# An S5 state-space layer and a SwiGLU layer side by side: the first chunk's state output as seven block products, and the up half-columns in two pairs at other places

## The chip, the cores and the metric

The kernel runs on one core of a Trainium2 chip. The metric is the device time of one execution in microseconds (us). TensorE (PE in the profile) multiplies matrices, VectorE (DVE) and ScalarE (ACT) do elementwise work, GpSimd (POOL) issues DMAs that add into their target and does a few small powers, and SyncE (SP) issues loads, stores and transposing DMAs.

## What is computed

The input `x` has 2048 rows (time steps) of 512 features. With `xn` the layer norm of `x`, the output is `x` plus an S5 state-space layer of `xn` plus a SwiGLU layer of `xn`:

```python
Bu = einsum("bld,pd->blp", xn, B_bar)            # complex, 512 states
h_t = Lam_bar * h_{t-1} + Bu_t                   # along the 2048 steps
y  = 2 * einsum("blp,dp->bld", h, C).real + xn * Dskip
f  = (silu(xn @ w_gate) * (xn @ w_up)) @ w_down  # F = 1376
out = x + y + f
```

## The kernel before

The 2048 rows are worked in four chunks of 512 columns (`NCH`, `CW`), each of four tiles of 128 rows. `xnT` holds `xn` transposed. For chunks 2 and 3 ACT normalizes the rows (L235) with a factor that is a power on POOL (L214) and a shift `nb` from DVE (L217), both once for a chunk; DMAs transpose the result. Ten products of constants (L828) run on PE before its first data. For each chunk there are these stages:

- **B projection** (`bproj_chunk`, products at L380): eight banks of PSUM, real and imaginary part of four state tiles. ACT casts each bank into `u` (L382).
- **State** (`ssm_ops`), on DVE: `u` is rotated by cosine and sine tables `c16` and `s16`, so that the recurrence becomes real; eight scans (L459); a small carry (L468 to L473); and a rotation back into the state `wt`. `rotation` has four products and two sums on DVE. `rotation_dma` has the four products alone, and POOL issues two DMAs that add one product into another (L426); it needs the negated sine table, which `negate_table` makes with four copies on ACT (L411).
- **Gate and up** (`gateup_chunk`): first the last feature tile (L550, evicted by L553 and L554), then ten feature tiles, each with a gate and an up bank (L492), evicted by ACT with silu (L511) and a cast (L512). DVE multiplies two tiles at a time (L507).
- **Last feature tile.** Of its 96 columns, 96 of gate and 32 of up are in the bank of L550. The other 64 columns of up are made for all four chunks at once by `up_halves` (L539), two chunks in a bank. DVE multiplies (L527), and `move_rows` has SP issue 12 small DMAs for each chunk that lay the product out for `out_rows` (L595).
- **Output** (`out_ffn`, L750, or L724 for the last pair): a PSUM bank for each tile of 128 rows gathers the products with `w_down`, then `out_rows`, then the state part.

The state part multiplies the state (real and imaginary) by C folded with its coefficients, `CF`. `CF` is made by `c_ops`: eight times a scaled copy on ACT (L363) and a DVE step (L366). There are two forms. `out_ssm` has 8 products of 512 columns for each tile (L762), 32 for a chunk. `out_ssm_seven` treats state and `CF` as 2 x 2 blocks and makes the product of a chunk from seven block products of 256 columns (L657, 56 products), by Winograd's form of Strassen's scheme. It needs sums of blocks. Those of `CF` (`t1` to `t4`, in place of `CT`) and those of the state (`s1` to `s4`) are made by signed copies on ACT (L606) and adding DMAs from POOL (L610), each in a chain of dependent steps. Two results go through ACT (L690, L693), and four adds and four final sums are on DVE (L669). Before, chunk 0 and chunk 3 use `out_ssm` and chunks 1 and 2 the seven products.

**What sets the order.** Each engine runs its instructions in the order in which the program gives them, and the program is written out by hand: the stages of PE follow each other as above, and the DVE work stands in a list, `backlog`, of steps with a cost. After each PE group `pump` adds the group's time to what is owed and takes steps from the list; `need(tag)` empties the list up to a tag; `multiply` takes waiting products; `spend` takes steps from the list `sums`. Where a step stands in the list therefore decides where it stands in each engine's queue. PE's order from the middle on is: gate and up of chunk 1, B projection of chunk 2, output of chunk 0 with `up_halves` and `out_ssm`, gate and up of chunk 2, B projection of chunk 3, output of chunk 1 with the seven products, gate and up of chunk 3, and `out_pair` for chunks 2 and 3. There are eight PSUM banks. The four output banks of chunk 0 stay taken from its output products until its last row products, which come with the output of chunk 1.

Of the kernel before, what the change touches and what calls it, by code (L numbers as in the profile page):

```python
# [23 lines left out]
def kernel(  # L24
# [382 lines left out]
    neg_s16 = xnT[:, :, 0:CW]  # L407

    def negate_table():
        for q in range(NQ):  # L410
            nc.scalar.activation(out=neg_s16[:, q], in_=s16[:, q], func=ACT.Copy, scale=-1.0)  # L411

    def rotation_dma(src, dst, back):

        box = {}
        sines = (s16[:], neg_s16) if back else (neg_s16, s16[:])

        def side(i):
            t = box[i] = ssm.tile([128, NQ, CW], BF16, name="pm", bufs=3)
            V.tensor_tensor(out=t[:], in0=src()[:, i], in1=sines[i], op=ALU.mult)  # L420
# [22 lines left out]
    def ssm_ops(c):  # L443
# [9 lines left out]
        ops = (rotation_dma if c == 3 else rotation)(lambda: u_tiles[c], lambda: u_tiles[c], False)  # L453
# [27 lines left out]
        back = (rotation_dma if c == 2 else rotation)(g, wt, True)  # L481
# [4 lines left out]
    u_pair = {}  # L486
    products = []
# [12 lines left out]
    def u_tile(c, fi):  # L500
        if (c, fi // 2) not in u_pair:
            u_pair[c, fi // 2] = up_p.tile([128, 2, CW], BF16, name="u2")
        return u_pair[c, fi // 2]

    def product(c, fi):
        g, u = gu_tile(c)[:, fi - 1:fi + 1, :], u_tile(c, fi)[:]
# [16 lines left out]
    def product_last(c):  # L523
        g, u = gu_last[c % 2][0:LB + LA, :], ul(c)[0:LB + LA, :]
        def mul():
            to = g if c == NCH - 1 else u
            V.tensor_tensor(out=to, in0=g, in1=u, op=ALU.mult)  # L527
            move_rows(c, to)
        products.append(mul)

    def up_halves():

        pss = []
        for c in range(0, NCH, 2):
            ps = bank()
            pss.append(ps)
            for k in range(KD):
                for i in range(2):
                    nc.tensor.matmul(ps[i * LB:(i + 1) * LB], lhsT=wu_last[:, k, :],  # L539
                                     rhs=xnT[:, k, (c + i) * CW:(c + i + 1) * CW], start=(k == 0), stop=(k == KD - 1))  # L540
        for c in range(NCH):
            i = c % 2
            nc.scalar.copy(out=ul(c)[0:LB, :], in_=pss[c // 2][i * LB:(i + 1) * LB])
        product_last(0)
        product_last(1)

    def gateup_last(c):
# [7 lines left out]
        if c > 1:  # L555
            product_last(c)
# [18 lines left out]
    def skip_add():  # L575
        V.tensor_tensor(out=xn_end[:], in0=xn_end[:], in1=xall[:, NT - TPC:NT, :], op=ALU.add)
# [23 lines left out]
    neg_b22 = BT[:, 1, :, 0:HD]  # L600
    parts = {NT - 1: part_end, NT - 2: jidx}

    def signed_copy(out, in_, sign):

        for lo in range(0, NQ, 2):
            yield lambda lo=lo: nc.scalar.activation(out=out[:, lo:lo + 2], in_=in_[:, lo:lo + 2], func=ACT.Copy,  # L606
                                                     scale=sign)

    def added(out, in_):
        yield lambda: nc.gpsimd.dma_start(out=out, in_=in_, accum_op=ALU.add)  # L610

    def weight_sums():
# [3 lines left out]
        for out, in_, sign, to, add in ((t3, b12, -1.0, t3, b22), (t1, b11, -1.0, t1, b12), (t2, b11, 1.0, t2, t3),  # L616
                                        (t4, b22, -1.0, t4, t1)):
            yield from signed_copy(out, in_, sign)
            yield from added(to, add)
        yield from added(t4, b21)  # L620
# [6 lines left out]

    def state_sums(c):

        (a11, a12), (a21, a22) = state_quarters(c)  # L630
        if c == 1:
            s1, s2, s3 = (ssm.tile([128, NQ, HW], BF16, name="cm", bufs=3) for _ in range(3))
            s4 = jidx[:].bitcast(BF16).rearrange("p (q j) -> p q j", q=NQ)
        else:
            s1, s2, s3, s4 = ((wg_g, wu_g)[i // 2][2][:, :, (i % 2) * HD:(i % 2 + 1) * HD] for i in range(4))
        s_tiles[c] = (s1, s2, s3, s4)
        for out, in_, sign, to, add in ((s1, a21, 1.0, s1, a22), (s3, a21, -1.0, s3, a11), (s2, a11, -1.0, s2, s1),
                                        (s4, a12, -1.0, s4, s2)):
# [471 lines left out]
```

## Time and profile before

| | us |
|---|---|
| three runs | 176.61, 176.98, 176.90 |
| median | 176.9 |
| profiled execution | 177.04 |
| its span, first to last instruction | 175.2 |
| PE busy | 171.7 (98%) |
| DVE busy | 161.1 (92%) |
| ACT busy | 107.6 (61%) |
| POOL busy | 45.9 (26%) |

PE's granted clock was 1.00 in the whole execution. In the chain of waits each piece is the work that the next piece waited for, back from the last instruction; in the timelines a row gives the start, the time from first start to last end, engine, line, operation, tiles and count, and in brackets how long the engine stood idle before it and what released it. The DMA view gives for each kind of transfer the size of one and the median time from issue to landing.

### The profile page before, as it was taken

The numbers are of one execution on the slowest core, as the hardware profiler recorded it, in microseconds if no ns is written. First come the engines' busy times: TensorE is split into PE (matmuls) and PEld (weight loads), VectorE is DVE, ScalarE is ACT, GpSimd is POOL, SyncE is SP. The second block draws the span as 40 slices with busy tenths as digits, with TensorE's granted clock in tenths as the row PEclk, the third lists the DMA queues.
The fourth block names the chain that finished last, engine by engine and source line by source line (L and its number), as shares of the span: only waits on it lengthen the run. The fifth ranks groups of instructions, "written<-read, shape, count | busy, mean of one in ns | idle before, by whom it ended". The sixth has DMA issues, their size and how long they took to land.

```text
span 175.2 us, 2790 instructions
## 1 busy us (share of the span) xinstructions
PE 171.7 (98%) x1002; PEld 88.4 (50%) x1002; DVE 161.1 (92%) x248; ACT 107.6 (61%) x204; POOL 45.9 (26%) x49
## 2 busy tenths in 40 slices
PE   8999999999999999999999999999999999999993
PEld 2977544444444444444444444468444444447743
DVE  4779998999999997999999999999999999995884
ACT  5487898868598669772998699052486691001100
POOL 6050120000400130000352224136544841211440
PEclk9999999999999999999999999999999999999999
DMA  6998496995332013700399449339898999955034
GB/s 170 294 170 226 91 250 117 362 230 121 77 76 30 0 30 75 254 4 11 43 105 120 60 51 194 61 60 136 139 156 153 157 175 192 122 60 60 0 105 139
DMA packets 38974, 21.36 MB, mean 122 GB/s; under 512 B 22016, under 2 KB 38144, under 8 KB 38944
## 3 DMA queue, kind: packets, MB, share of 16 engines
q0 software_dynamic: 9552, 8.26, 34.0%
q1 hardware_dynamic: 28016, 12.30, 31.1%
q10 hardware_dynamic: 1392, 0.62, 1.3%
q8 instruction: 8, 0.13, 0.3%
q14 instruction: 6, 0.05, 0.1%
HBM read 8.33 MB, written 4.19 MB: 71 GB/s over the span
## 4 chain that ended last, share of the span: by engine, by line
PE 98%; DVE 0%; issue 0%
PE ps L492 35%; PE ps L380 16%; PE ps L724 10%; PE ps L750 10%; PE ps L762 8%; PE ps L657 7%; PE ps L851 2%; PE ps L828 2%; PE ps L550 2%; PE ps L932 2%; PE ps L595 2%; PE ps L539 1%; PE ps L245 1%; DVE res L767 0%; PE ps L275 0%
## 5 line engine op out<-in xcount | busy, mean ns | idle before, releaser
L492 PE MATMUL ps<-xnT,wg 128*128 128x512 bf16 (+1 forms) x148 | 36.6, 373 | 0.0
L492 PE MATMUL ps<-xnT,wu 128*128 128x512 bf16 (+1 forms) x148 | 36.6, 373 | 0.0
L459 DVE TENSOR_TENSOR_SCAN g<-r_t,car,u 128x512 bf16<-128x512 f32 x24 | 28.7, 1264 | 0.0
L380 PE MATMUL ps<-xnT,BT 128*128 128x512 bf16 x128 | 28.3, 379 | 0.0
L511 ACT ACTIVATE guT<-ps 128x512 bf16<-128x512 f32 (+1 forms) x40 | 24.0, 599 | 5.4 <-PE ps L492 3.4
L512 ACT CAST u<-ps 128x512 bf16<-128x512 f32 (+1 forms) x40 | 23.3, 583 | 4.7 <-PE ps L492 4.5
L492 PEld LDWEIGHTS <-wu 128*128 128x128 bf16 x148 | 14.5, 98 | 16.6
L492 PEld LDWEIGHTS <-wg 128*128 128x128 bf16 x148 | 14.4, 98 | 16.5
L382 ACT CAST u<-ps 128x512 bf16<-128x512 f32 x32 | 18.2, 586 | 4.0 <-PE ps L380 3.9
L380 PEld LDWEIGHTS <-BT 128*128 128x128 bf16 x128 | 12.5, 98 | 14.9
L750 PE MATMUL ps<-wd_sb,guT 128*128 128x512 bf16 x80 | 17.6, 379 | 0.0
L724 PE MATMUL ps<-wd_sb,guT 128*128 128x512 bf16 x80 | 17.4, 379 | 0.0
L214 POOL TENSOR_TENSOR rstd<-ve,neg_half 128x2 f32<-128x2 f32 (+1 forms) x4 | 5.7, 1415 | 44.9 <-DVE ve L213 44.9
L762 PE MATMUL ps<-CF,wt 128*128 128x512 bf16 (+2 forms) x80 | 14.2, 336 | 0.0
L507 DVE TENSOR_TENSOR guT<-guT,u 128x1024 bf16<-128x1024 bf16 x20 | 13.4, 679 | 0.0
L724 PEld LDWEIGHTS <-guT 128*128 128x128 bf16 x80 | 7.8, 98 | 9.4
L750 PEld LDWEIGHTS <-guT 128*128 128x128 bf16 x80 | 7.8, 98 | 9.4
L205 DVE BATCH_NORM_STATS2 stats<-xall 128x6 f32<-128x512 bf16 x14 | 9.5, 679 | 2.0 <-DMA xall<-in_A_x_dram 2.0
L610 POOL DMA_DIRECT2D CT<-CF x3 | 3.9, 1300 | 27.1 <-ACT CT L606 23.6
L690 ACT COPY guT<-ps 128x512 f32<-128x512 f32 x2 | 1.2, 586 | 15.8 <-PE ps L657 15.8
L762 PEld LDWEIGHTS <-wt 128*128 128x128 bf16 x80 | 7.1, 98 | 6.9 <-issue 0.4
L459 DVE TENSOR_TENSOR_SCAN g<-r_t,u 128x512 bf16<-128x512 f32 x8 | 9.3, 1205 | 0.0
(168 smaller groups left out, 265.0 us busy)
## 6 DMA issues: line engine op xcount, KB each, us to landing
wd_sb<-in_B_w_down_dram SPq DMA_DIRECT2D x2, 640.0 KB, 8.7
xall<-in_A_x_dram SPq DMA_DIRECT2D x1, 1024.0 KB, 6.2
out_dram<-res POOLq DMA_DIRECT2D x8, 128.0 KB, 3.8
wt<-pm POOLq DMA_DIRECT2D x2, 512.0 KB, 5.4
u<-pm POOLq DMA_DIRECT2D x2, 512.0 KB, 6.2
out_dram<-xall POOLq DMA_DIRECT2D x2, 512.0 KB, 10.2
CT<-CF POOLq DMA_DIRECT2D x3, 256.0 KB, 4.3
gu_rows<-ul SPq DMA_DIRECT2D x36, 8.0 KB, 1.8
```

Source lines behind the costliest of these rows:

```text
L205: nc.vector.bn_stats(out=stats[:, n, :], in_=xall[:, n, :])
L380: nc.tensor.matmul(ps[:], lhsT=BT[:, part, k, q * 128:(q + 1) * 128], rhs=xnT[:, k, c * CW:(c + 1) * CW], start=(k == 0), stop=(k == KD - 1))
L382: nc.scalar.copy(out=u_tiles[c][:, part, q, :], in_=ps[:])
L459: V.tensor_tensor_scan(out=g()[:, part, q, :], data0=r_t[:, q:q + 1].to_broadcast([128, CW]), data1=u_tiles[c][:, part, q, :], initial=ini ...
L492: nc.tensor.matmul(ps[:fs, lo:hi], lhsT=wslice(groups, fi, k), rhs=xnT[:, k, c * CW + lo:c * CW + hi], start=(k == 0), stop=(k == KD - 1))
L507: products.append(lambda: V.tensor_tensor(out=g, in0=g, in1=u, op=ALU.mult))
L511: nc.scalar.activation(out=gu_tile(c)[:, fi, 0:hi], in_=psg[:, 0:hi], func=ACT.Silu)
L512: nc.scalar.copy(out=u_tile(c, fi)[:, fi % 2, 0:hi], in_=psu[:, 0:hi])
L657: nc.tensor.matmul(place(i), lhsT=a[:, q, i * 128:(i + 1) * 128], rhs=b[:, q, :], start=(start and q == 0), stop=(stop and q == NQ - 1))
L724: nc.tensor.matmul(o[:], lhsT=gu_tiles[k][:, fi, i * 128:(i + 1) * 128], rhs=wd_sb[:, fi, :], start=(fi == 0), stop=False)
L750: nc.tensor.matmul(o[:], lhsT=gu_tiles[c][:, fi, i * 128:(i + 1) * 128], rhs=wd_sb[:, fi, lo:hi], start=(fi == 0), stop=False)
L762: nc.tensor.matmul(o, lhsT=w_tiles[c][:, part, q, i * 128:(i + 1) * 128], rhs=CF[:, part, q, lo:hi], start=(fresh and part == 0 and q == 0 ...
```

## The change

- Chunk 0's `out_ssm` goes. Its output banks stay open, and `out_ssm_seven(0)` runs behind the B projection of chunk 3, with chunk 0's row products; the sums of chunk 1's state are written out there too, ahead of it.
- The state sums of chunk 0 start inside the list of `c_ops` (`sums_begin`, after the first C step), and the sums of `CF` follow it (`sums_go_on`, then `leftover`). Signed copies with sign +1 become plain DMA copies from SP (or from ACT's queue for chunk 1); the order of all sums is new, and the last operand is no longer negated separately.
- `up_halves` becomes `up_pair(0)`, ahead of the B projection of chunk 2, and `up_pair(2)`, ahead of that of chunk 3, with their products and row moves.
- Chunk 0's rotation back and chunk 1's rotation forward use `rotation_dma` too. The negated sine table moves to `part_end` and `jidx` and is made during gate and up of chunk 1, one copy for a feature tile.
- `skip_add` becomes an adding DMA; the skip products of the chunks come in the order 3, 2, 0, 1; the stores of chunks 0 and 1 move into `out_pair`, and the state sums of chunk 2 behind its first output tile.
- The copy of `x` to the output moves ahead of `up_pair(0)`, `load_rows` behind the B projection of chunk 3. The up tiles `u2` become slices of one tile `u_all`, whose space chunk 0's seven products use.

The core of the diff:

```diff
-    neg_s16 = xnT[:, :, 0:CW]
+    neg_s16 = [t[:].bitcast(BF16).rearrange("p (q j) -> p q j", q=2) for t in (part_end, jidx)]
...
-        ops = (rotation_dma if c == 3 else rotation)(lambda: u_tiles[c], lambda: u_tiles[c], False)
+        ops = (rotation_dma if c in (1, 3) else rotation)(lambda: u_tiles[c], lambda: u_tiles[c], False)
...
-        back = (rotation_dma if c == 2 else rotation)(g, wt, True)
+        back = (rotation_dma if c in (0, 2) else rotation)(g, wt, True)
...
-    def up_halves():
...
+    def up_pair(c):
+
+        ps = bank()
+        for k in range(KD):
+            for i in range(2):
+                nc.tensor.matmul(ps[i * LB:(i + 1) * LB], lhsT=wu_last[:, k, :],
+                                 rhs=xnT[:, k, (c + i) * CW:(c + i + 1) * CW], start=(k == 0), stop=(k == KD - 1))
+        for i in range(2):
+            nc.scalar.copy(out=ul(c + i)[0:LB, :], in_=ps[i * LB:(i + 1) * LB])
...
     def skip_add():
-        V.tensor_tensor(out=xn_end[:], in0=xn_end[:], in1=xall[:, NT - TPC:NT, :], op=ALU.add)
+        nc.gpsimd.dma_start(out=xn_end[:], in_=xall[:, NT - TPC:NT, :], accum_op=ALU.add)
...
     def weight_sums():
...
+        yield from copied(t4, b21, pieces=2)
+        yield from negated(t1, b11)
+        yield from added(t1, b12)
+        yield None
+        yield from negated(t2, b22)
+        yield from added(t2, t1)
+        yield from negated(t3, b12)
+        yield from added(t3, b22)
+        yield from added(t4, t2)
...
     def state_sums(c):
...
+        s1, s2, s3, s4 = s_tiles[c] = [t[:] for t in state_places(c)]
+        q = nc.scalar if c == 1 else nc.sync
+        yield from negated(s2, a22)
+        yield from copied(s4, a12, q)
+        yield from copied(s1, a21, q)
+        yield from negated(s3, a21)
+        yield from added(s3, a11)
+        yield from added(s1, a22)
+        yield None
+        yield from added(s2, s3)
+        yield from added(s4, s2)
...
     def out_pair(c):
 
         multiply(0)
         for n in [*parts, *range(c * TPC, NT - len(parts))]:
             o_tiles[n] = [bank()]
-        for op in state_sums(c):
-            op()
         for n in range(c * TPC, (c + 2) * TPC):
+            if n == c * TPC + 1:
+                need("skip")
+                for _, op in filter(None, state_sums(c)):
+                    op()
+                skip_store(0)
+                skip_store(1)
...
     def out_chunk(c):
...
         if c == 0:
-            need("ln3")
-            up_halves()
-            negate_table()
-            multiply(0)
-        if c == 1:
-            for step in range(3):
-                for k in range(2):
-                    out_rows(k, step)
-            for n in range(TPC):
-                out_leave(n, o_tiles[n][0], opool.tile([128, D], BF16, name="res"))
+            need("cf")
+            sums.extend(leftover)
+            spend(4)
+            return
+        for k in range(3):
+            out_rows(c, k)
         need(f"ssm{c}")
-        need("cf")
-        if c == 1:
-            spend(99, True)
-            return out_ssm_seven(c)
-        for n in range(c * TPC, (c + 1) * TPC):
-            out_ssm(n)
-            pump(2 * NQ * 0.2163)
+        out_ssm_seven(c)
...
-    fwd1, back1, _ = ssm_ops(1)
-    queue("ssm1", fwd1 + back1)
+    fwd1, back1, turns = ssm_ops(1)
+    queue("ssm1", fwd1[:turns])
...
+    cf = c_ops()
+    queue("cf", cf[:1] + [(0.0, sums_begin)] + cf[1:] + [(0.0, sums_go_on)])
+    queue("ssm1", fwd1[turns:] + back1)
+    sums += negate_table()
     gateup_chunk(1)
+    nc.sync.dma_start(out=out[0, 0:(NT - 2 * TPC) * 128, :], in_=A_x[0, 0:(NT - 2 * TPC) * 128, :])
+    up_pair(0)
+    product_last(0)
+    product_last(1)
     nc.gpsimd.dma_start(out=dsk_bc[:], in_=A_Dskip.partition_broadcast(128))
     bproj_chunk(2)
-    nc.sync.dma_start(out=out[0, 0:(NT - 2 * TPC) * 128, :], in_=A_x[0, 0:(NT - 2 * TPC) * 128, :])
     queue_ssm(2)
     out_chunk(0)
-    sums += [*weight_sums(), None]
     gateup_chunk(2)
+    up_pair(2)
+    product_last(2)
     bproj_chunk(3)
+    load_rows()
+    need("ssm1")
+    spend(99)
+    sums.extend(filter(None, state_sums(1)))
+    spend(99)
+    out_ssm_seven(0)
+    move_rows(2, ul(2))
```

More of the change, by code (lines that the diff above doesn't have):

```diff
@@ L962, with spend @@
     sums = []
-    def spend(n, late=False):
-        while n and sums:
-            if sums[0] is None:
-                if not late or any(item[3] == "ssm1" for item in backlog):
-                    return
-                sums[0:1] = state_sums(1)
-            sums.pop(0)()
-            n -= 1
+    def spend(n):
+        while sums and sums[0][0] <= n:
+            cost, op = sums.pop(0)
+            op()
+            n -= cost
     def bproj_chunk(c):
```

129 lines of the change are left out of this document (63 added, 66 removed).

## The prediction

> **What bounds the kernel now.** I read the page's busy shares first, then the chain of waits in order of time, then the timelines of ScalarE (ACT), VectorE (DVE), GpSimd (POOL) and the DMA queue of SyncE around the places that the change touches. In the chain each row is start, length, engine, tile, line, count.
>
> ```profile
> PE 171.7 (98%) x1002; PEld 88.4 (50%) x1002; DVE 161.1 (92%) x248; ACT 107.6 (61%) x204; POOL 45.9 (26%) x49
> ```
> ```profile
> 56.70 6.91 PE ps L380 x32
> 63.60 8.63 PE ps L750 x40
> 72.24 1.85 PE ps L539 x16
> 74.09 7.01 PE ps L762 x32
> ...
> 81.96 17.27 PE ps L492 x80
> ...
> 116.17 6.22 PE ps L657 x56
> ...
> 140.53 17.27 PE ps L724 x80
> 157.79 1.41 PE ps L595 x24
> 159.20 6.36 PE ps L657 x56
> ```
>
> The chain is TensorE (PE) alone, one stage beginning where the last ended: it has no gap. Whatever is saved on PE is saved outright, and every gap that a change opens is paid in full. DVE is the second bound: 161.1 us of work, and at the end only just ahead (below). The sum is made against the profiled execution, 177.04 us with a span of 175.2; the median of the runs shown is 176.9, 0.14 lower, and I end on that.
>
> **What the change saves on PE.** Chunk 0's state output was 32 products of 512 columns, 7.01 us (L762). Seven block products are 56 of 256 columns; the kernel already has them for chunk 1, 6.22 us, and chunk 2, 6.36 us. Saved: 7.01 - 6.22 = 0.79 us. The up half-columns (L539, 16 products, 1.85) become two pairs of 8, 0.92 each: nothing gained or lost. The third pass of the row products (L595) is regrouped, not changed. So the change can give 0.8 us; the question is whether PE stays without a gap.
>
> **Where PE comes to wait: the start of chunk 2's gate and up.** Before, 1.85 + 7.01 us of PE work lay between the output products of chunk 0 (L750) and gate and up of chunk 2, and ACT used them to catch up. Both are gone from there. By the new order PE ends gate and up of chunk 1 at 56.70 as now, runs the first up pair to 57.62, the B projection (6.91) to 64.53, the output products (8.63) to 73.16, and starts chunk 2 at once. Four of the eight PSUM banks hold chunk 0's unfinished outputs until the seven products, so four are left: the last feature tile, gate 0, up 0 and gate 1 take them, four times 4 x 0.216 = 0.86 us, until 76.6. Up 1 takes the bank of the last feature tile, and waits for ACT to have emptied it. ACT's queue is in order, so I follow what stands before that.
>
> ```profile
> 56.93 1.22 DVE L390 TENSOR_TENSOR pm<-g,c 128x2048 bf16<-128x2048 bf16 x1
> 58.06 0.68 DVE L205 BATCH_NORM_STATS2 stats<-xall 128x6 f32<-128x512 bf16 x1
> ...
> 59.99 0.69 DVE L507 TENSOR_TENSOR guT<-guT,u 128x1024 bf16<-128x1024 bf16 x1
> ...
> 69.24 4.07 DVE L366 SCALAR_TENSOR_TENSOR CF<-CT,nc2im,cm 128x512 bf16<-128x512 bf16 x6 [0.56 <-ACT cm L363]
> ...
> 77.89 0.75 DVE L527 TENSOR_TENSOR ul<-gu_last,ul 96x512 bf16<-96x512 bf16 x2
> ```
> ```profile
> 45.23 0.65 POOL L1063 DMA_DIRECT2D dsk_bc<-in_A_Dskip_dram  x1
> 60.85 1.92 POOL L214 TENSOR_TENSOR rstd<-ve,neg_half 128x4 f32<-128x4 f32 x1 [14.97 <-DVE ve L213]
> ...
> 121.00 0.85 POOL L426 DMA_DIRECT2D wt<-pm  x1 [0.64 <-DVE wt L423]
> ```
> ```profile
> wt<-pm POOLq DMA_DIRECT2D x2, 512.0 KB, 5.4
> ```
>
> DVE's order is the same until 56.93. Then it has a rotation product (1.13 to the next start), statistics and the second product (58.06 to 59.99 with one of each: 1.93), which makes the first DMA join ready at 60.0; two gate products (0.6 each), the two last-tile products moved up (0.7), two half products for the second side (0.6 each): 63.2. The chunk 3 shift `nb` waits for POOL's power, which now stands behind that join's issue (0.4 to start, 0.85) and the Dskip load moved there (0.65): 60.0 + 0.4 + 0.85 + 0.65 + 1.92 = 63.9, against 62.8 before. Then DVE's product for the second join ends at 65.2, three more rotation steps and two halves come, and the C products L366 start at 70.0 (66.6 before), 0.67 each.
>
> ```profile
> 64.19 0.81 ACT L235 ACTIVATE xn_end<-xall,nb,rstd 128x512 bf16<-128x512 bf16 x1
> 64.91 1.06 ACT L382 CAST u<-ps 128x512 bf16<-128x512 f32 x2
> 65.85 0.73 ACT L363 ACTIVATE cm<-CT,c2re 128x512 f32<-128x512 bf16 x1
> 66.47 0.81 ACT L235 ACTIVATE xn_end<-xall,nb,rstd 128x512 bf16<-128x512 bf16 x1
> ...
> 82.00 0.59 ACT L553 ACTIVATE gu_last<-ps 96x512 bf16<-96x512 f32 x1 [4.26 <-PE ps L550]
> 82.61 0.58 ACT L554 CAST ul<-ps 32x512 bf16<-32x512 f32 x1
> 83.21 1.15 ACT L606 ACTIVATE CT<-CF 128x512 bf16<-128x512 bf16 x2
> ```
>
> ACT from 64.1 (after `nb`): four norms (0.72 each), two casts (0.47), three scaled copies L363 (0.62): 69.8. Now the four new negations of chunk 0's state quarters (0.55 each, from L606's pair): two until 70.9; the other two wait for the second join, issued at 65.6 and landing 5.4 later, 71.0. They end at 72.1. The five other L363 stand behind them, each of which a C product waits for: the fourth C product starts at 72.8, the eighth ends at 72.8 + 5 x 0.67 = 76.2. ACT's next negations, of C's quarters, wait for that eighth; three of them stand ahead of the last feature tile: 76.2 + 1.65 = 77.9. Then its two evictions, 0.61 + 0.60: 79.1. **PE waits from 76.6 to 79.1: 2.5 us.** Before, ACT stood idle 4.26 us ahead of the same eviction. One more negation comes before gate 0's eviction, which ends at 79.1 + 0.55 + 0.6 = 80.25, while PE is through up 1 at 80.0: 0.3 more. After that ACT needs 1 us a tile and PE 1.73, so it ends. Bounds: no less than 2.4 + 0.2 if the join lands so early that only ACT's own queue counts; with a landing 1.1 us longer 3.6 + 0.3. The Trainium skill ("DMA: Bandwidth & Descriptors", section "Anatomy of one DMA") fits GpSimd's DMAs with 2.0 us plus bytes at 436 KB a us, an estimated 3.2 for 512 KB; the row has 5.4 and I use the row; by the page the wait would lie at the lower bound.
>
> **The later stages and the end.** With gate and up of chunk 2 (0.86 + 17.27), the second up pair (0.92) and the B projection (6.91) after 73.16, the first seven products start at 99.1 + 2.8 = 101.9. The new adds cost DVE what the old seven cost:
>
> ```profile
> 109.58 8.31 DVE L459 TENSOR_TENSOR_SCAN g<-r_t,car,u 128x512 bf16<-128x512 f32 x7
> 117.81 0.13 DVE L468 TENSOR_TENSOR ct<-g,cos 128x4 f32<-128x4 bf16 x1
> ...
> 120.62 0.68 DVE L669 TENSOR_TENSOR guT<-ps,guT 128x512 f32<-128x512 f32 x1
> ...
> 123.53 2.48 DVE L669 TENSOR_TENSOR res<-ps,guT 128x512 bf16<-128x512 f32 x4
> 125.93 1.21 DVE L420 TENSOR_TENSOR pm<-g,xnT 128x2048 bf16<-128x2048 bf16 x1
> ...
> 157.58 1.23 DVE L404 TENSOR_TENSOR wt<-pm 128x2048 bf16<-128x2048 bf16 x1
> 159.25 0.69 DVE L734 TENSOR_TENSOR part_end<-ps,xn_end 128x512 f32<-128x512 f32 x1 [0.45 <-PE ps L595]
> ```
>
> From 76.2 DVE has eight scans (1.18 each), a carry (0.5), eleven rotation steps (1.2) and six small products (3.3) ahead of these adds, and comes to them at 102.6; the first block product that they need ends at 101.9 + 3 x 0.89 = 104.6, so PE's temporary banks come free in time.
>
> The adds are 120.62 to 125.93, 5.3 us more for DVE; four rotation products and the skip sum (now a DMA), each of the 1.2 us of L390's row, are 6 us less. So DVE's sum stays, but its order does not: from the last add of chunk 1's seven to L734 it had 125.93 to 158.75, 32.8 us, and 0.45 to spare. Now the carry and two rotation products (117.81 to 120.62, 2.8 us) come after those adds, and the skip sum (1.2) goes: 34.4. PE goes from the end of those seven products (E, 116.17 + 6.22 = 122.4) to the end of L595 (159.2) in 36.8. The last four adds cannot start before E and take 2.4; with DVE about 0.3 late there L734 starts at E + 37.1. It frees the bank that PE's second block product of chunk 2 needs 0.89 into the stage: 37.1 + 0.69 - 36.8 - 0.89 is just over 0. I take 0.2 (0 to 0.8).
>
> The sum: -0.79 + 2.5 + 0.3 + 0.2 = +2.2 us. **177.04 + 2.2 = 179.2; as median 176.9 + 2.2 = 179.1 us.**
>
> Costed at nothing: the four negations of the sine table now lie in chunk 1's gate and up, where all eight banks turn over (without that cover 2.2 us); the DRAM copy of `x` moves ahead of the row moves in SP's queue and runs while no product waits for a DMA.
>
> **Rivals.** (a) *The sums come late.* The sums for the first seven are now chains of DMAs, behind others in two queues.
>
> ```profile
> 63.84 5.97 SPq L259 DMA_TRANSPOSE xnT<-xn_end  x4
> ...
> 78.33 26.18 SPq L188 DMA_DIRECT2D gu_rows<-ul  x36
> 131.03 14.61 SPq L188 DMA_DIRECT2D gu_rows<-gu_last  x12
> ```
> ```profile
> L610 POOL DMA_DIRECT2D CT<-CF x3 | 3.9, 1300 | 27.1 <-ACT CT L606 23.6
> ...
> CT<-CF POOLq DMA_DIRECT2D x3, 256.0 KB, 4.3
> ```
>
> On SP 24 row moves (0.73 each, 17.5 us from 62) and four transposes (6) come before the copies that the sums start from: issued at 85.5 and landed at 90. POOL takes its adds in order, and from there t4 needs two issues (1.3 each) and three landings of 4.3 one after another, 15.5 us: 105.5. PE wants it 5 x 0.89 = 4.5 us into the stage, at 106.4. It fits by 0.9 us; each us later than that costs one, as does chunk 2's s2 behind the last 12 moves (14.6 us). For it: the margin. Against it: row moves took as little as 0.6 us each in the first stretches. It gives 180 to 182; I take 181.
>
> (b) *PE's clock falls in the gap.*
>
> ```profile
> 0.78 3.78 PE ps L828 x10
> ```
>
> These warm-up products, eight of 512 columns and two of 128, would take 1.8 us at 0.216 per 512 columns; they take 3.78. A PE that goes back to that state pays some 2 us again: 181.1. For it: before, PE never stopped, so nothing here shows how long it may. Against it: the gap is short. The Trainium skill ("TensorE: Matmul & The Clock Gate", section on the HAM clock gate) has the clock halved after an idle window of about 3.4 us: by it my 2.5 us would pass and the 3.6 of the upper bound might not. No run here shows it yet.
>
> (c) *Not slower: ACT is ahead after all.* The place is the eviction of chunk 2's last feature tile; it decides at 76.6. If ACT is through by then, because join, C products and negations together run 2.5 us faster than their rows, nothing is paid but the end: 176.9 - 0.8 + 0.2 = 176.3. For it: ACT has 39% idle time overall. Against it: the steps are in-order sums of measured rows, and all of them must be too long. That the seven products do not save what they say is not in doubt beyond 0.15 us, by the two rows of them.
>
> **How the numbers follow.** Forecast 0.66 (178.2 to 180.8: its bounds and half a us for the rows' spread); (a) 0.10 and (b) 0.07, both slower; (c) 0.17, of which 0.11 is faster by over 0.2% (0.35 us, about what a measurement of this kernel can tell from no change) and 0.06 within it. So faster 0.11, same 0.06, slower 0.83. The range leaves out (c) and the top of (a): 177.7 to 181.4.
>
> **What would show it.** In the chain of waits after: the state output of chunk 0 at 6.2 us; a stretch not of PE ahead of the second up product of chunk 2, with ACT's eviction of the last feature tile (L555) as releaser, 2 to 3.6 us; ACT idle for the join (DMA) and for DVE's L366 before it; granted clock 1.00 in the stage. At the end L761 starting at or after the end of L596. If PE has no gap near 77 us the forecast falls; if the gap is there and the time is above 180.5, look at waits for DMA ahead of the seven products, and at the clock.

## The result, and where the time went

After the change the median is 188.1 us (187.99, 186.79, 188.25, 188.21), before 176.94 on the same chip: ratio 1.061, 95% interval 1.056 to 1.067. The profiled execution took 187.99 with a span of 186.2, 11.0 more than the span before. Slower was forecast, but by 2.2 us, to 179.1.

The page of the changed kernel, busy shares and two lines of the 40 slices (4.66 us each):

```profile
PE 172.9 (93%) x1012; PEld 90.6 (49%) x1026; DVE 160.1 (86%) x255; ACT 103.7 (56%) x194; POOL 55.2 (30%) x57
...
PE   7999999999999999699999169999999999999992
...
PEclk9999999999999999999999958999999999999998
```

TensorE (PE) has almost the same work, but two holes: a small one in slice 17 (near 77 us) and a large one in slices 23 and 24 (near 105 to 112), with the clock down behind it. PE's timeline at both, and the granted clock (the column ahead of the last two) in stretches of 4 us:

```profile
75.29 1.03 PE L498 MATMUL ps<-xnT,wg 128*128 128x512 bf16 x4
77.92 1.02 PE L498 MATMUL ps<-xnT,wu 128*128 128x512 bf16 x4 [1.60 <-ACT ul L555]
79.20 1.02 PE L498 MATMUL ps<-xnT,wg 128*128 128x512 bf16 x4 [0.25 <-ACT guT L517]
...
101.00 1.91 PE L682 MATMUL ps<-CF,wt 128*128 128x256 bf16 x16
108.87 4.88 PE L682 MATMUL ps<-CT,xnT 128*128 128x256 bf16 x24 [5.96 <-DMA CT<-CT]
113.82 1.03 PE L682 MATMUL ps<-CT,wt 128*128 128x256 bf16 x8
...
115.66 0.83 PE L596 MATMUL ps<-BT,gu_rows 32*128 32x512 bf16 x12
```
```profile
104.00:108.00 4.00, 0.00 (x0) 0.00 (x0) 0.00 (x0) 0.90 (x2) 0.67 (x1) 0.80 1.18 190
108.00:112.00 4.00, 3.13 (x15) 2.19 (x16) 0.69 (x1) 0.00 (x0) 2.98 (x3) 0.50 0.79 91
```

The first hole is the one that was forecast, 1.85 us instead of 2.8. The second is rival (a): chunk 0's seven products wait for the sums `t2` and `t4` of `CF`. The stage goes from 101.00 to 115.66, 14.66 us. The queues of SP and POOL say why:

```profile
61.23 20.91 SPq L188 DMA_DIRECT2D gu_rows<-ul  x24
82.25 6.07 SPq L259 DMA_TRANSPOSE xnT<-xn_end  x4
88.42 1.44 SPq L612 DMA_DIRECT2D xnT<-wt  x2
```
```profile
92.65 1.28 POOL L615 DMA_DIRECT2D xnT<-wt  x1 [19.99 <-DMA xnT<-wt]
93.41 1.83 POOL L615 DMA_DIRECT2D xnT<-xnT  x1
94.15 2.39 POOL L615 DMA_DIRECT2D CT<-CF  x1
99.51 1.28 POOL L615 DMA_DIRECT2D xnT<-xnT  x1 [2.97 <-DMA xnT<-xnT]
102.08 1.28 POOL L615 DMA_DIRECT2D CT<-CT  x1 [1.29 <-DMA BT<-in_B_w_down_dram]
102.83 1.84 POOL L615 DMA_DIRECT2D CT<-CF  x1
109.02 1.28 POOL L615 DMA_DIRECT2D CT<-CT  x1 [4.35 <-DMA CT<-CT]
```

SP issues 24 row moves and four transposes, and only then the copy that `s1` starts from. POOL takes its additions in order, so it stands for 20 us at `s1`, and with it the sums of `CF` behind it, whose first copies ACT had made by 76.8. The rows at 94.15, 102.08, 102.83 and 109.02 are `t1`, `t2`, `t3` and `t4`. `t2` needs `t1` and `t4` needs `t2`; `t3` only stands between them in the queue. The DMA view gives the median time from issue to landing, of `t1` and `t3` and then of `t2` and `t4`:

```profile
CT<-CF POOLq DMA_DIRECT2D x2, 256.0 KB, 7.5
CT<-CT POOLq DMA_DIRECT2D x2, 256.0 KB, 5.7
```

One by one it is 7.4 for `t1`, 6.7 for `t2` and 4.8 for `t4`. So `t1` landed at 101.55, `t2` at 108.78, where PE's wait ends, and `t4` at 113.82, where the products that need it begin. (The bracket at 102.08 names the load of `w_down`'s rows, which `t2` doesn't read; what the half microsecond between the landing of `t1` and this issue was, the profile doesn't show.)

Up to the first product of chunk 3's gate and up (132.04, before 122.23) the change loses 9.81 us, from there to the end of the last product (182.49, before 172.50) 0.18, and from there to the end of the span 3.7 instead of 2.7.

### The profile page after: what moved, and what is told of

It reads as the page before. It is cut to its first block, busy times and chain, and to the rows that moved or that the text cites. A ratio compares the mean times of both kernels' runs of the same rounds, so it can differ in the third digit from the quotient of the medians.

```text
span 186.2 us, 2859 instructions
## 1 busy us (share of the span) xinstructions
PE 172.9 (93%) x1012; PEld 90.6 (49%) x1026; DVE 160.1 (86%) x255; ACT 103.7 (56%) x194; POOL 55.2 (30%) x57
## 4 chain that ended last, share of the span: by engine, by line
PE 46%; DVE 29%; DMA 6%; ACT 6%; issue 5%; POOL 3%; SPq 1%; DVEq 0%; POOLq 0%
PE ps L498 17%; PE ps L753 9%; PE ps L682 8%; DVE g L464 5%; PE ps L777 5%; DVE stats L205 4%; PE ps L789 3%; DVE pm L315 3%; DMA CT<-CT 3%; DVE guT L513 3%; DVE pm L390 2%; DMA xall<-in_A_x_dram 2%; DMA BT<-in_B_w_down_dram 2%; PE ps L380 2%; ACT xn_end L235 2%
## 5 line engine op out<-in xcount | busy, mean ns | idle before, releaser
L518 ACT CAST u_all<-ps 128x512 bf16<-128x512 f32 (+1 forms) x40 | 23.1, 579 | 5.1 <-PE ps L498 5.1
L777 PE MATMUL ps<-wd_sb,guT 128*128 128x512 bf16 x78 | 17.5, 379 | 0.1
L513 DVE TENSOR_TENSOR guT<-guT,u_all 128x1024 bf16<-128x1024 bf16 x20 | 13.3, 677 | 0.0
L682 PE MATMUL ps<-CT,xnT 128*128 128x256 bf16 x32 | 5.9, 363 | 6.0 <-DMA CT<-CT 6.0
L615 POOL DMA_DIRECT2D xnT<-wt x3 | 4.4, 1475 | 20.7 <-DMA xnT<-wt 20.0
L711 POOL DMA_DIRECT2D out_dram<-res x8 | 7.6, 1624 | 7.5 <-DVE res L694 7.5
L682 PEld LDWEIGHTS <-xnT 128*128 128x128 bf16 x48 | 5.6, 119 | 7.8 <-issue 6.2
```

The lines of the kernel that those rows point to most:

```text
L513: products.append(lambda: V.tensor_tensor(out=g, in0=g, in1=u, op=ALU.mult))
L518: nc.scalar.copy(out=u_tile(c, fi)[:, fi % 2, 0:hi], in_=psu[:, 0:hi])
L682: nc.tensor.matmul(place(i), lhsT=a[:, q, i * 128:(i + 1) * 128], rhs=b[:, q, :], start=(start and q == 0), stop=(stop and q == NQ - 1))
L711: nc.gpsimd.dma_start(out=out_v[:, n, :], in_=res[:], accum_op=ALU.add)
L777: nc.tensor.matmul(o[:], lhsT=gu_tiles[c][:, fi, i * 128:(i + 1) * 128], rhs=wd_sb[:, fi, lo:hi], start=(fi == 0), stop=False)
```

## Experiments

Theory A: the sums are late because of the place of their first copies in SP's order. Against it: the additions are too slow wherever they begin (B), the row moves hold them up by their traffic (G), and the slow clock is a cost of its own (C). Theory E gives the first hole to ACT's queue, F the longer end to the two late skip stores, H what is left to DVE. Each ratio is against the kernel before on the same chip, with its 95% interval.

### Rows late (theory A against B)

```diff
-            if c != NCH - 2:
+            if c == NCH - 1:
                 move_rows(c, to)
...
     out_chunk(0)
+    move_rows(0, ul(0))
+    move_rows(1, ul(1))
```

> The 24 row moves of chunks 0 and 1 are issued on SP behind the copies for the sums instead of ahead of them; nothing else differs from the changed kernel. Theory A (the sums are late because SP issues their copies behind 20.9 us of row moves): the copies of s1 are issued some 20 us earlier than 88.4, TensorE no longer waits 5.96 us for t2 at 108.9, the granted clock stays at 1.00, and the median falls from 188.1 by 6.0 + 2.2 = 8.2 to about 180, with 1.85 (the wait for ACT at 77) and 1.4 (the end) still there. Theory B (eight additions in POOL's one queue take too long wherever they begin): the first additions come earlier, but t4 still lands after 110 and the median stays above 186.

179.1 us, ratio 1.012 (1.008 to 1.016): 9.0 less than the changed kernel, from the order of one queue. SP and PE of this kernel:

```profile
64.19 7.49 SPq L259 DMA_TRANSPOSE xnT<-xn_end  x4
71.79 3.04 SPq L612 DMA_DIRECT2D xnT<-wt  x2
74.93 2.85 SPq L612 DMA_DIRECT2D CT<-CF  x2
77.83 22.27 SPq L188 DMA_DIRECT2D gu_rows<-ul  x24
```
```profile
101.11 1.91 PE L682 MATMUL ps<-CF,wt 128*128 128x256 bf16 x16
102.86 2.78 PE L682 MATMUL ps<-CT,xnT 128*128 128x256 bf16 x24
...
107.32 0.83 PE L596 MATMUL ps<-BT,gu_rows 32*128 32x512 bf16 x12
```

The stage begins as in the changed kernel and takes 6.21 instead of 14.66: the second hole was 8.45 us in all. B falls. The first hole (1.57 + 0.25) is still there. In the changed kernel the DMA engines were nearly idle for part of the time for which the copies stood in line, from 77.6 to 84 us; their busy share from 76 to 92 us in 40 slices of 0.4 us:

```profile
DMA  9999210010010012000009207604901910499999
```

### One chunk's rows late (how much of it)

```diff
-            if c != NCH - 2:
+            if c in (0, NCH - 1):
                 move_rows(c, to)
...
     out_chunk(0)
+    move_rows(1, ul(1))
```

> Only chunk 1's 12 row moves are issued behind the copies, chunk 0's 12 stay ahead of them. With theory A the delay is one of issue time on SP: 12 moves of 0.87 us end near 72 instead of 82, the copies go out some 6 us later than with none ahead (71.8) and 10 us earlier than with 24 (88.4); t2 then lands near 101 and t4 near 106.5, so TensorE waits 0 to 1.5 us and the median is 179 to 180.5. Rival (a threshold elsewhere, such as the transposes of chunk 3 or the traffic of the rows): the wait for t2 or t4 is more than half of the 5.96 us, and the median is above 183.

179.45 us, ratio 1.015 (1.013 to 1.018), as by A. Its SP queue:

```profile
61.50 10.06 SPq L188 DMA_DIRECT2D gu_rows<-ul  x12
...
80.41 1.46 SPq L612 DMA_DIRECT2D xnT<-wt  x2
```

The copies go out at 80.4, between 71.8 and 88.4, and that is soon enough: no wait for `CT` is listed any more.

### The copies on POOL, the rows in place (A against G)

```diff
-        q = nc.scalar if c == 1 else nc.sync
+        q = (nc.gpsimd, nc.scalar, nc.sync)[c]
...
-        yield from copied(t4, b21, pieces=2)
+        yield from copied(t4, b21, nc.gpsimd, pieces=2)
```

> The row moves stay where the changed kernel has them, ahead on SP; only the four copies for chunk 0's sums and for t4 go to POOL's queue instead of SP's. Theory A (what made the sums late is the place of the copies in SP's order, nothing else): s1 is copied near 72 instead of 88.4, the wait for t2 at 108.9 is gone, and the median is within 1.5 of the kernel with the rows moved late, so 179 to 181. Rival G (the 24 row moves hold up the additions by their traffic or by sharing the DMA engines, and moving them later helped by that): copies and additions still land late while the moves run, TensorE still waits 3 us or more, and the median stays above 183.

185.2 us, ratio 1.049 (1.045 to 1.054): neither number. In the trace the sums are early with all row moves in place, which is A's mechanism and speaks against G: the last addition, for `t4`, goes out at 95.95 instead of 109.02, and PE doesn't wait for a sum. But the next transfer in SP's line is now awaited, the transposes of chunk 3, by the second up pair. POOL, PE's waits and SP's queue:

```profile
95.95 1.27 POOL L615 DMA_DIRECT2D CT<-CT  x1 [3.28 <-DMA CT<-CT]
```
```profile
PE ps L543 <- DMA xnT<-xn_end: 4.5, 1, 4.5
```
```profile
61.20 24.41 SPq L188 DMA_DIRECT2D gu_rows<-ul  x24
85.72 8.34 SPq L259 DMA_TRANSPOSE xnT<-xn_end  x4
```

So it is the row moves' issue time that others pay for, whoever stands behind; here they took 1.02 us each, with the copies running beside them, and the transposes came 3.5 us later than in the changed kernel, where they were in time. The clock adds to it: behind the wait it is 0.50 from 98 to 102 us, and the B projection of chunk 3 takes 8.3 us instead of 6.9.

### Keeping the clock up in the hole

```diff
-        six = taken(s2, t2)
+        six = bank((128, 2, HD))
+        if c == 0:
+            for _ in range(24):
+                nc.tensor.matmul(six[:].rearrange("p i j -> p (i j)"), lhsT=ones[:, 0:128], rhs=ones, start=True, stop=True)
+        product(s2, t2, lambda i: six[:, i, :], True, True)
```

> 24 spare products of 512 columns (ones by ones) go into the sixth product's bank ahead of it, so that TensorE works through the wait for t2; they add work and change no result. Theory C (the clock of 0.50 behind the gap is a cost of its own): the 24 products behind the gap go from 4.88 to about 2.7 us and the median falls by 2.2 to about 185.9. Theory D (t4, which landed at 113.77, was binding anyway, so the slow products lay inside its wait): a wait for t4 of about 2 us opens behind them instead, and the median stays at 188.1 within 0.4.

188.9 us, ratio 1.065 (1.059 to 1.072): no gain. PE of this kernel:

```profile
103.31 5.41 PE L719 MATMUL ps<-const-bfloat16-1.0 128*128 128x512 bf16 x23
108.97 2.90 PE L682 MATMUL ps<-CT,xnT 128*128 128x256 bf16 x24 [0.25 <-DMA CT<-CT]
114.13 1.86 PE L682 MATMUL ps<-CT,wt 128*128 128x256 bf16 x8 [2.26 <-DMA CT<-CT]
```

The 24 products run at full clock in 2.90 instead of 4.88, and PE waits 2.26 for `t4` instead. So C falls for the changed kernel: there the slow clock lay inside the wait for `t4`, which alone dated the stage. In this kernel the clock falls behind that wait, and the last 16 products pay for it (below).

### The first hole, and the same rule met again

The remaining negations come one per tile of chunk 2's gate and up:

```diff
             sums.extend(leftover)
-            spend(4)
             return
```

> The negations that ACT got in one go behind chunk 0's output rows are spread, one per tile of chunk 2's gate/up stage. Theory E (the gap at 77 is ACT's: its two copies of the last feature tile stand behind three negations): the waits of 1.60 and 0.25 on ACT go, and the median falls by 1.6 to 1.85 to about 186.4, since the later sums wait for SP in any case. Rival (the gap is DVE's last products of C, which the negations follow): the wait stays, and the median stays at 188.1 or rises because t2 and t3 come later.

187.4 us, ratio 1.058 (1.054 to 1.062). Both waits on ACT are gone, so E holds for the hole. But PE only comes to the sums 1.6 us earlier (99.39) and waits there for 8.7 us instead of 5.96. My 186.4 was wrong to count the gain as kept while a later wait dates the stage.

The same with the rows late, and two negations per tile:

```diff
-            spend(1)
+            spend(2 if c == 2 else 1)
```

> Rows moved late as in the first experiment, and chunk 0's remaining negations two per tile behind the evictions of chunk 2's first gate/up tiles instead of in one go ahead of them. Theory E (the remaining wait of 1.60 and 0.25 at 77 is ACT's): both go, the sums have some 5 us in hand and stay in time, and the median falls from 179.1 by 1.6 to 1.9 to about 177.3, that is no different from the kernel before. Rival: t2 and t3 come too late by the delay of the negations, a wait for CT opens at 103 to 106, and the median stays at 179 or above.

Ratio 1.034 (1.028 to 1.039): a hole again, and again SP's order (4.48 us in this profile, 3.4 in that of the same kernel without two stores, below). The dropped `spend(4)` had also issued the copies for `t4`; now they stood behind the row moves in the program. SP and PE:

```profile
75.46 23.55 SPq L188 DMA_DIRECT2D gu_rows<-ul  x24
99.11 1.41 SPq L612 DMA_DIRECT2D CT<-CF  x2
```
```profile
109.14 1.87 PE L682 MATMUL ps<-CT,wt 128*128 128x256 bf16 x8 [4.48 <-DMA CT<-CT]
```

The same with those copies ahead of the rows (a `spend` that takes only steps that cost ACT nothing):

```diff
             sums.extend(leftover)
+            spend(0)
             return
```

> As the kernel with rows late and negations spread, except that the two copies for t4 are given to SP ahead of the 24 row moves (in that kernel they had come behind them, at 99.1, and t4 was awaited for 4.48 us). Theory A: both waits are then gone, the one for ACT at 77 (1.85 us) and the one for t4, and the median falls from 179.1 (rows late alone) by 1.6 to 1.9 to about 177.3: within 0.3% of the kernel before. Rival: the negations, two per tile, still make t3 or t4 late, a wait for CT stays, and the median is 179 or more.

179.25 us, ratio 1.012 (1.009 to 1.015). PE's list of waits now names neither ACT nor a sum, and the median doesn't fall below that of the rows late alone. The gain is there at its place: from the last feature tile of chunk 2 to the B projection it is 19.8 us, and 21.4 with the rows late alone. In the profiled execution two things take it back: a wait of 0.81 for DVE at the end (next section), and 0.9 that lies ahead of all that was changed (the first up pair begins at 57.23 instead of 56.30; 0.5 of it is a wait for a load of the up weights). The second is not in the profile of the same kernel as control below, so it says nothing about the edit.

### Is the seven-product form worth it in good order?

The last kernel with plain products for chunk 0 and no state sums for it:

```diff
...
-    out_ssm_seven(0)
+    for n in range(TPC):
+        out_ssm(n)
+        pump(2 * NQ * 0.2163)
+    for k in range(3):
+        out_rows(0, k)
+    for n in range(TPC):
+        out_leave(n, o_tiles[n][0], opool.tile([128, D], BF16, name="res"))
```

> As the kernel of this group with copies first, but chunk 0's state output by the eight plain products at the same place (no state sums, no block additions, four ACT copies out of PSUM; other work is handed to DVE behind each product as in the kernel before). If the seven products gain 7.01 - 6.22 = 0.79 us on TensorE and nothing takes it back: 0.8 above the kernel with seven products, about 178.1. Rival: DVE, freed of 8 additions (4 of them in four block sums, 5.3 us in all), is no longer late at L761 and the sums' DMAs are gone, and the plain products are equal or faster.

177.6 us, ratio 1.0045 (1.003 to 1.006): the plain products are 1.6 us faster than the seven in good order, though their stage takes 7.00 us of PE instead of 6.21. Rows of DVE show one reason, of the seven products with copies first and then of the plain ones:

```profile
105.50 0.69 DVE L694 TENSOR_TENSOR u_all<-ps,u_all 128x512 f32<-128x512 f32 x1 [2.15 <-ACT u_all L715]
...
161.18 0.68 DVE L761 TENSOR_TENSOR part_end<-ps,xn_end 128x512 f32<-128x512 f32 x1
```
```profile
159.61 0.69 DVE L761 TENSOR_TENSOR part_end<-ps,xn_end 128x512 f32<-128x512 f32 x1 [4.62 <-PE ps L596]
```

With plain products DVE is 4.62 us ahead there; with the seven it comes late and PE waits 0.81 for it. Its eight additions of chunk 0 and the 2.15 us for which it stands among them, waiting for ACT, lie in the same queue ahead of L761.

An earlier form of the plain version lacked the `pump` and stood beside the kernel with the copies for `t4` behind the rows:

> As the kernel with rows late and negations spread, but chunk 0's state output by the eight plain products at the same place, with no state sums, no block additions on DVE, and four ACT copies to leave PSUM. If seven products are worth 7.01 - 6.22 = 0.79 us of TensorE and nothing else: 0.8 above that kernel, about 178.1. Rival: their 5.6 us of additions on DVE and their DMAs cost as much where DVE is just late at L761, and the two are equal or the plain products faster.

181.1 us, ratio 1.027 (1.024 to 1.030) against 1.034 (1.028 to 1.039), with DVE idle for 7.99 us for want of the `pump`. The intervals overlap, and the seven products of this pair have the wait for `t4`, so the pair says little about the two forms.

Three tries at this (theory H): two additions left out, one multiplication ahead of L761 left out, and two more steps given to DVE where it stood idle, the last two beside an unchanged control. The edits are `if c > 0:` ahead of the additions of `five` into `low[:, :, 1]` and `high[:, :, 1]`; and

```diff
...
-            box[3] = mul(1, c16)
+            box[3] = box[1] if c == NCH - 1 and back else mul(1, c16)
```
```diff
+        if c == 0:
+            step()
+            step()
         add(u2, six[:], low[:, :, 0])
```

> As the kernel with copies first, with two of the eight block additions of chunk 0 left out (those that add the fifth product into one half block of each row pair, 0.69 us each on DVE; the right halves of chunk 0's rows come out wrong). Theory H (DVE sets the end: L761 begins 0.81 us late because DVE has 5.6 us of additions more than with plain products): L761 begins 1.4 us earlier against the products, the wait of 0.81 goes, and the ratio to the kernel before falls from 1.0118 by 0.0046 to about 1.007. Rival (the loss lies elsewhere, in TensorE's stages): the wait or the time stays, ratio 1.010 or more.

> As the kernel with copies first, with one of the four multiplications of the last rotation (chunk 3's, 1.22 us on DVE, shortly ahead of L761) left out, so the second part of chunk 3's rotated state is wrong. Theory H (DVE's L761 holds up TensorE at the end): L761 begins when the row products end, the wait of 0.8 us goes, and the median is 0.8 below that of the unchanged version on this chip. Rival (something else sets the end): equal within 0.3.

> The kernel with rows late, negations spread and the copies for t4 first, unchanged, as the point to measure the other two from: 177.7 to 179.5, with TensorE's wait for L761 of 0.8 to 1.1 us.

> As the kernel with copies first, but DVE is given the next two operations of its list (the last of chunk 1's... chunk 2's and 3's order unchanged, some 2.4 us in all) ahead of chunk 0's first block addition, where it stood idle 2.15 us for the copy of the fifth product. Theory H: DVE is up to 2 us earlier from there on, the wait for L761 goes, and the median is 0.8 below the unchanged version, about 178.4, still above the kernel before. Rival (the additions begin later, PSUM banks come free later): a new wait of TensorE at 106 to 112 and no gain.

| | median | ratio |
|---|---|---|
| two additions less | 180.1 | 1.017 (1.013 to 1.020) |
| one multiplication less | 178.6 | 1.0105 (1.008 to 1.013) |
| control | 178.8 | 1.011 (1.008 to 1.015) |
| two steps more | 179.0 | 1.011 (1.009 to 1.014) |

None is faster than the control by more than the intervals; the first was run on another chip than the other three. In it DVE spent what it had won (1.4) on waiting, 0.74 for the row products and 0.94 for a transfer in POOL's queue, and L761 still held PE up for 1.05:

```profile
133.76 1.23 DVE L425 TENSOR_TENSOR pm<-u,s 128x2048 bf16<-128x2048 bf16 x1 [0.94 <-DMA wt<-pm]
```

In the second PE's wait for L761 (0.55 in the control) is gone from the profile, and the profiled span is 1.0 shorter, but that execution is the fastest of its five, and the medians differ by 0.2, less than their intervals. In the third that wait is gone too; PE waits for the rows of `w_down` instead, which SP issues behind the 24 row moves (at 101.12, 1.3 us later than in the control):

```profile
106.81 1.31 PE L596 MATMUL ps<-BT,gu_rows 32*128 32x512 bf16 x10 [0.67 <-DMA BT<-in_B_w_down_dram]
```

So H is right about the wait, and not shown as the price of 1.6 us between seven and plain products. For the two profiled executions, the control's (span 176.7) and that of the plain products (175.7), the stages add up: the seven products save 0.71 between the B projection of chunk 3 and chunk 3's gate and up, and lose 0.71 from the last row products to the last product (the wait for L761 among them), 0.60 behind the last product, 0.24 in chunk 2's gate and up, and 0.17 ahead of the change. These are single executions, and runs of the seven products spread from 177.7 to 180.1, so how the medians share it stays open.

### The end

On the changed kernel the skip stores go back behind their products:

```diff
-                skip_store(0)
-                skip_store(1)
...
-        queue("skip", [(1.2, lambda c=c: skip_op(c))] + {3: [(0.0, skip_add)], 2: [(0.0, lambda: skip_store(2))]}.get(c, []))
+        queue("skip", [(1.2, lambda c=c: skip_op(c))] + [(0.0, skip_add if c == 3 else lambda c=c: skip_store(c))])
```

> The skip stores of chunks 0 and 1 (512 KB each, on POOL's queue) are issued behind their products as in the kernel before, instead of behind the last sums. Theory F (they share the DMA engines and POOL's queue with the last output stores): from the last product to the end of the span goes from 4.1 back to about 2.7 us, and the median falls by 1.4 to about 186.7. Rival (the end is the later skip work of DVE): the end stays at 4.1 and the median at 188.1.

194.9 us, ratio 1.100 (1.095 to 1.106): neither time, though the end did go back, from 3.7 to 2.8 us. The two stores now fall among the copies and additions for chunk 2's sums; the copy that `s1` starts from landed in 11.5 us and not in about 5, and PE waits for the last sum:

```profile
wg<-wt SPq DMA_DIRECT2D x1, 256.0 KB, 11.5
```
```profile
PE ps L682 <- DMA wg<-wu: 5.4, 1, 5.4
```

On the seven products with copies first, the two stores are left out (the first two lines of that diff alone):

> As the kernel with copies first, but without the skip stores of chunks 0 and 1 (those rows lack the term x times D). Theory F (the last output stores land late because these two stores of 512 KB land beside them): the stores of the end land in 1.7 us as in the kernel before, and the median is 0.3 to 1.4 below that kernel. Rival: equal within 0.2 us.

178.5 us, ratio 1.009 (1.007 to 1.012). From the end of the last product to the end of the span it is 2.7 (173.80 to 176.5), as in the kernel before, against 3.2 with the stores. The same edit on the kernel with two additions less:

> As the kernel with two additions less, and without the skip stores of chunks 0 and 1 besides (their rows lack x times D). Theories H and F together: the wait for DVE and the slow stores of the end both go; the two gains add to 0.8 + 0.6 = 1.4 us below the kernel with copies first, ratio about 1.004. That would be the most that the seven products can reach here: no faster than the kernel before. Rival: below 0.998, so that a version of the change can win.

178.9 us, ratio 1.011 (1.009 to 1.014) against 1.017 (1.013 to 1.020) with the stores, and 2.7 behind the last product instead of 3.7. It is no 1.004, since H's part did not come. A third pair, on the kernel with the copies for `t4` behind the rows, gave 1.033 (1.029 to 1.036) against 1.034 (1.028 to 1.039), with that kernel's hole in both and 2.75 behind the last product instead of 3.0:

> As the kernel with rows late and negations spread, but the skip stores of chunks 0 and 1 (two additions of 512 KB into the output) are left out, so those rows lack the term x times D. Theory F (the end of the changed kernel is longer because these stores land beside the last output stores): the time behind the last product falls from 3.0 - 3.7 to 2.7 or less, and the median is 0.3 to 1.4 below that kernel. Rival: the end does not move, and the two are equal within 0.2.

So F holds for the end in the profiles: without the two stores it is 2.70 to 2.75 in three kernels, with them late up to 3.99. It isn't a fixed price, since two profiles with the stores late have 2.69 (one chunk's rows late) and 2.77 (negations spread, rows in place). In the times it isn't resolved: the medians of the first two pairs are 0.8 and 1.2 apart with intervals that overlap, and the third pair is equal.

Last, the diff of the skip stores on the plain version:

> The plain-product version with the skip stores of chunks 0 and 1 back behind their products. There POOL is idle from 134 to 144 and the sums of chunk 2 begin at 144. If the stores land before the copies of those sums go out at 145: the end is as in the kernel before, and the ratio falls from 1.0045 by 0.001 to 0.002 to about 1.003. If they collide with the copies and sums as in the experiment with the changed kernel (the copy that the sums need landed in 11.5 us instead of about 5): TensorE waits for a sum of chunk 2 at 165 and the ratio is above 1.01.

178.2 us, ratio 1.007 (1.005 to 1.009), with no wait for a sum and 2.9 behind the last product: neither number, not told apart from the plain products with late stores, and no faster. No version was faster than the kernel before; the plain products with rows late come nearest.

## Why the prediction was wrong, step by step

- **The saving, -0.79: right.** The stage takes 6.21 with seven products and 7.00 with plain ones at the same place.
- **The wait at chunk 2's gate and up, 2.5 + 0.3: right in place and cause, 1.60 + 0.25 in size,** below the 2.4 + 0.2 that I had called the least. The whole chain came 0.7 to 1.2 us earlier than my sum: POOL's power began at 61.20 (forecast 61.9), `nb` followed at 63.05 and ACT's norms at 63.24 (64.1), the C products began at 69.12 (70.0), the eighth ended at 75.1 (76.2), ACT was through at 77.9 (79.1), while PE was only 0.45 earlier. The least had taken ACT's start from the same sum. ACT's four negations ran in one go (68.87 to 71.05), so the 0.1 us that I had it wait for the second join did not come either. DVE and ACT of the changed kernel:

```profile
69.12 2.07 DVE L366 SCALAR_TENSOR_TENSOR CF<-CT,nc2im,cm 128x512 bf16<-128x512 bf16 x3
71.70 3.40 DVE L366 SCALAR_TENSOR_TENSOR CF<-CT,nc2im,cm 128x512 bf16<-128x512 bf16 x5 [0.51 <-ACT cm L363]
...
169.28 0.68 DVE L761 TENSOR_TENSOR part_end<-ps,xn_end 128x512 f32<-128x512 f32 x1
```
```profile
68.87 2.18 ACT L606 ACTIVATE xnT<-wt 128x512 bf16<-128x512 bf16 x4
...
75.13 1.67 ACT L606 ACTIVATE CT<-CF 128x512 bf16<-128x512 bf16 x3 [0.50 <-DVE CF L366]
...
77.29 0.58 ACT L555 CAST ul<-ps 32x512 bf16<-32x512 f32 x1
```
- **DVE at the end, +0.2: right.** L761 began 37.1 behind the end of chunk 1's seven products (132.2 to 169.28), as forecast, and PE lost 0.18.
- **The step that failed is "It fits by 0.9 us" in rival (a),** and with it the 0.10 for that rival. Three terms erred, all to one side. The row moves took 20.91 instead of 17.5 (0.87 each, from rows of 0.73), so the copies landed at 92.6 instead of 90. From there to `t4` I had two issues and three landings, 15.5 us, with 4.3 for each landing, the median of transfers that mostly stood alone (two others of that size in the same view of before took 9.4 and 9.5); it took 21.1 (92.65 to 113.8), with landings of 7.4 for `t1`, the third of three additions issued in one go, 6.7 for `t2` and 4.8 for `t4`. And PE would have wanted `t4` at 105.4 (4.4 into the stage, as with the rows late), not at 106.4. Together 8.45 us of stage, where (a) had been given up to 3. A margin of 0.9 behind 24 issues and a chain of transfers was no margin.
- **Rival (b), the clock:** the clock fell not at the first hole, where (b) had it, but inside the wait for `t4`, and there it cost nothing.
- **The end, costed at nothing: 1.0.** The two stores of the skip part, moved behind the last sums, are on their way beside the last output stores, which land in 3.5 us instead of 1.9 (in other profiles with these stores late the end is 0 to 1.3 longer than before). I had counted the move of `skip_add` and not of these two.

The sum with the measured terms: -0.79 + 1.85 + 8.45 + 0.18 + 1.0 = 10.7, of 11.0. The other 0.3 is a balance of small terms, read from start to start of PE's rows: the two up pairs take 2.16 instead of 1.85 and the row products 1.51 instead of 1.41, both costed at nothing; the first hole takes 2.19 and not the 1.85 of its brackets; and this execution was 0.46 earlier than the one before at the end of chunk 1's gate and up.

## What to carry to other kernels

A queue that issues DMAs is an engine with its own busy time: count all that stands ahead of a new transfer, at the price per issue of that place, and give a chain of transfers a margin in proportion to its length. When one waiter is helped, name who stands next in the same queue; here it was the transposes, the copies for `t4` and the rows of `w_down`, one after the other. Time saved on the first engine can be lost again where the second one loses its lead: here 0.71 of each, in two profiled executions.

## What the hardware showed that was not expected

- Row moves of 8 KB cost SP 0.87 us each to issue (1.02 in one run), and more when the DMA engines were busier. In the changed kernel it was 0.68 from 77.4 to 82.1, with a busy share of 0.07 from 78 to 82, and 1.18 and 1.31 in the two stretches from 69.9 to 77.4, at 1.05 and 1.04. The kernel before issued its first 12 at 0.64 with a share of 0.06 (78 to 86), and the 0.73 of the forecast was an average over such stretches.
- Of three additions of 256 KB that POOL issued 0.75 us apart, each landed later than the one ahead of it: 4.4, 5.8 and 7.4 us after its own issue in the changed kernel (from 92.65), 4.6, 5.9 and 7.3 with the rows late (from 81.14).
- The clock stayed at 1.00 behind a wait of 1.60. Behind the wait of 2.26 for `t4` in the kernel that kept PE busy, directly behind products at full clock, 16 products of 256 columns took 3.5 us instead of the 1.8 with the rows late; its window from 115 to 116 us:

```profile
115.00:116.00 1.00, 1.00 (x6) 0.67 (x5) 0.00 (x0) 0.00 (x0) 0.00 (x0) 0.50 1.30 147
```

The Trainium skill ("TensorE: Matmul & The Clock Gate", section on the HAM clock gate) puts the idle window at about 3.4 us; here less was enough.
